# A fused linear-attention and MLP kernel: the first merge of a new block behind the next chunk's products, five constant products, and one group's transposes one step later

## The chip, the cores and the metric

The kernel runs on one core of one Trainium2 chip. The metric is device time in microseconds (us) of one launch; the figure of a version is the median of its runs. The trace comes from one further execution, taken by the hardware profiler. Engines: PE is TensorE (PEld its weight loads), DVE is VectorE, ACT is ScalarE, POOL is GpSimd, SP issues the DMA transfers.

## The reference, cut to what matters

```python
# attention: 4 batches x 8 heads, 768 steps, head size 48
k_n = k / (np.linalg.norm(k, axis=-1, keepdims=True) + 1e-06)
for t in range(S):
    y[:, :, t] = einsum('bhd,bhde->bhe', q[:, :, t], state)
    v_old = einsum('bhde,bhd->bhe', state, k_n[:, :, t])
    state = state + beta[t] * einsum('bhd,bhe->bhde', k_n[:, :, t], v[:, :, t] - v_old)
# first MLP on x [4, 768, 384]
u = x + real(fft(fft(x, axis=1), axis=2))
un = normalized(u)                       # mean 0, variance 1 over 384 features
x = u + max(un @ w_ch1, 0) @ w_ch2       # 384 -> 1536 -> 384
# second MLP with a gate across positions
h = max(x @ w_in, 0);  u, v = halves of h
v_s = w_spatial @ normalized(v) + b_spatial
out = (u * v_s) @ w_out
```

## The kernel before, in words

The recurrence is computed in chunks of 64 steps. There are 4 batches x 12 chunks = 48 chunks, each with all 8 heads, in the order `SEQ` (a new batch begins every four chunks, so several batches are under way at once). A chunk needs the inverse of a triangular 64 x 64 matrix for each head. It is found as two 32 x 32 inverses on DVE (`solve`), for a block of eight chunks at once, and the part below the diagonal is put together by small products on PE (`merge`).

The main loop of `attention` runs over `t` from -3 to 47. One pass holds, on PE, in this order:

- `stage_d(t)`: the output and the new state of chunk t. 32 products take the chunk's values `WU` (the first half), then 32 take the corrected queries `cw` and the state `Sb` (the second half). `cw` is a DVE subtraction in `stage_c`; if it is late, PE stands between the two halves. A chunk that begins a batch has no second half.
- where `t % 8 == 5` and for t = -3 (so at t = -3, 5, 13, 21, 29 and 37): the first merge of a new block, `merge(..., True, False)`: 16 products (L483) on 32 x 32 corners that need `Tc`, the transposed inverses which `solve` writes with two DVE transposes (L352). ACT then writes `ZS` (L487) and copies the diagonal corners (`diag`, L469).
- `stage_c(t+1)`, eight products for the corrections (L532), interleaved pair by pair with `stage_a(t+20)`, eight key products (L224) for a chunk 20 ahead. ACT and DVE copy the result of L224 out (L199, L200). `stage_a` has nothing to do near the end, `stage_c` nothing for a chunk that begins a batch, as for t+1 = 5 and t+1 = 14.
- `stage_b(t+2)` (L517), and at odd t the second part of a merge (L485), which reads `ZS`.

The program's order on each engine is fixed as written (`chain` ties every instruction to the one before it on its engine). The DVE work of `solve` is cut into pieces and spread over the passes by the `part` calls; it is finished at the beginning of the passes t = 13, 21 and 29, just ahead of the merge.

From t = 37 on the Fourier transforms of the finished batches and the conversion of the weights fill in beside the attention. Then follow the first MLP and the second. In the first MLP two groups of 384 positions run interleaved: step `n` is L972 (to the hidden layer), then `between`, then nine products of L985 (back from it). `CF["stats"]` says at which `n` the groups 1 and 2 take their next preparation step, the first tuple of a pair ahead of L972, the second between L972 and L985. A step of group 2 is: statistics, rstd, normalize (`un`, L938 on ACT), then for each of three 128-feature pieces three transposes on PE (L957) and the copies out (L893 on ACT, L894 on DVE).

`halves` holds a helper of its own named `rows` (L413): it multiplies 32 columns of the identity with 288 columns of the mask `mk` and the result is never read.

Of the kernel before, what the change touches and what calls it, by code (L numbers as in the profile page):

```python
# [23 lines left out]
NBC = B * NC  # L24
# [6 lines left out]
HEAD = 24  # L31
# [13 lines left out]
CF = dict(  # L45
    skew=4, ring=20, kq=5, qt=3, mb=2, cvd=3, cve=2, kn=4,
    warm=8, keep=1, last=1, cuts=(0.5, 0.65), dfs=(1, 1, 1, 1, 2, 2, 3, 1, 2, 2, 3, 0), cvt=(0, 0, 0, 1, 2, 2, 1, 1, 0, 0, 0, 0), early=5, first=8, ahead=3,
    turns=(4, 6, 7, 9, 10, 12, 13, 15, 16, 16, 17, 17, 18, 18, 19, 20), stats=(((0, 1, 2, 3, 3), (2,)), ((21, 22, 22), (23, 24, 25))),
)

BANKS0 = dict(X=3, Y=4, Z=1)
# [15 lines left out]
class Kernel:  # L67
# [51 lines left out]
    def attention(self, cp, pg, pe, p, x, filler, after_solves):  # L119
# [345 lines left out]
        def diag(g8):  # L465

            o = (g8 % 4) * 8
            for h, us in enumerate(up):
                (nc.vector.tensor_copy if light(2 * g8 - 3) else nc.scalar.copy)(  # L469
                    out=TT[g8 % NTT][us, :, C * h + 32 : C * h + C], in_=Tts[g8 // 4][us, o : o + 8]  # L470
                )

        def merge(g8, first, second):

            z0, z1 = zz[:, g8 % 2 * 256 : g8 % 2 * 256 + 256].rearrange("p (g n) -> p g n", g=8), zz.rearrange("p (g n) -> p g n", g=8)
            T0, o0 = (Tts[g8 // 4] if first else None), (g8 % 4) * 8
            T1, o1 = (Tts[(g8 - 1) // 4] if second else None), ((g8 - 1) % 4) * 8
            tt = TT[(g8 - 1) % NTT]
            for g in range(8):
                for h in range(2):  # L480
                    if first:
                        ga = gas[g8 * 2 + g // 4][:, g % 4]
                        nc.tensor.matmul(z0[lo[h], g], lhsT=ga[up[h], C : C + 32], rhs=T0[up[h], o0 + g], start=True, stop=True)  # L483
                    if second:
                        nc.tensor.matmul(z1[up[h], g], lhsT=T1[lo[h], o1 + g], rhs=ZS[(g8 - 1) % 2][lo[h], g], start=True, stop=True)  # L485
            if first:
                nc.scalar.mul(ZS[g8 % 2][:96, :, 32:], z0[:96], -1.0)  # L487
            if second:
                for h in range(2):
                    nc.scalar.copy(out=tt[lo[h], :, C * h : C * h + C], in_=z1[up[h]])  # L490
# [31 lines left out]
        def stage_c(bc):  # L522
            qt = qts.pop(bc)
            if SEQ[bc][1] == 0:
                return
            w = st[bc][0]
            cw = p.tile([112, HP, 112], F32, name="cw", bufs=2)
            pc = self.bank("pc", [128, HP, 112])
            for hp in range(HP):
                for h in hs:  # L530

                    nc.tensor.matmul(pc[h, hp], lhsT=w[h, hp, :C], rhs=gas[bc][h, hp, : C + D], start=True, stop=True)  # L532
                yield
            nc.vector.tensor_sub(cw, qt, pc[:112])  # L534
            st[bc][1] = cw

        def stage_d(bc):

            b, c = SEQ[bc]
            wu, cw = st.pop(bc)  # L540
            sb = Sb[b]
            po, ps = self.bank("pd", [128, HP, D]), None
            if c < NC - 1:
                ps = self.bank("pd", [128, HP, D])

            for last in (False, True)[: 1 + (c > 0)]:
                for hp in range(HP):
                    begin, end = (not last and hp == 0, last and hp == HP - 1) if c else (True, True)
                    for i, h in enumerate(hs):

                        k, u, n = (cw[ds[i], hp], sb[ds[i], hp], C + D) if last else (gas[bc][h, hp], wu[h, hp, D:], 2 * C)
                        if ps is not None:
                            nc.tensor.matmul(ps[C * i : C * i + n - C, hp], lhsT=k[:, C:n], rhs=u, start=begin, stop=end)  # L553
                        nc.tensor.matmul(po[hs[1 - i], hp], lhsT=k[:, :C], rhs=u, start=begin, stop=end)  # L554
            if c == HALF:
                px = self.bank("pb", [128, HP, 2, D])
                xr = p.tile([1, DM], F32, name="xr", bufs=2)
                for i in range(2):
                    for hp in range(HP):
                        nc.tensor.matmul(px[C * i : C * i + 1, hp, i], lhsT=qx[ds[i], b, hp : hp + 1], rhs=sb[ds[i], hp], start=True, stop=True)  # L560
            if c < NC - 1:
                nc.scalar.copy(out=sb, in_=ps)
            if c == HALF:
                for i in range(2):
                    nc.scalar.copy(out=xr.rearrange("p (h t d) -> p h t d", h=HP, t=2)[:, :, i], in_=px[C * i : C * i + 1, :, i])
                st["x", b] = xr
            cc = c if c < HALF else NC - 1 - c
            js = slice(64 * (cc % 2), 64 * (cc % 2) + 64)
            tl = cc // 2 + (0 if c < HALF else 3)
            for i in range(2):  # L570
                nc.scalar.copy(out=x[b][js, tl].rearrange("p (h t d) -> p h t d", h=HP, t=2)[:, :, i], in_=po[hs[1 - i]])
            if c == NC - 1:
                nc.scalar.copy(out=x[b][0:1, 3], in_=st.pop(("x", b)))
# [77 lines left out]
        for t in range(T0, NBC):  # L651
            if t in STARTS:
                if solver:
                    solver.finish()
                j, span, total = STARTS[t]
                solver, since = Spread(solve(j), total), t
            part = (lambda f: solver.upto(SECOND(t + f) if j == 1 else (t - since + f) / span)) if solver and not light(t) else (lambda f: None)
            if light(t) and solver:
                solver.finish()
                solver = None  # L660

            if 0 <= t + 2 < NBC and (not light(t) or (t + 2) % 8 == 0) and not sooner(t + 2):
                values(t + 2)
            for bc in ahead.get(t, ()):
                mask_q(bc)
            if t - since < span - 1:
                part(c1)
            if t >= 0:
                stage_d(t)
                if SEQ[t][1] == NC - 1:  # L670
                    fill.extend(filler(SEQ[t][0]))
            new = t % 8 == 5 and t + 3 < NBC
            if new:

                merge((t + 3) // 2, True, False)
                load_kv(t + 3)
                if t >= LAST:
                    load_kv(t + 4)
                diag((t + 3) // 2)
            corrected = stage_c(t + 1) if 0 <= t + 1 < NBC else iter(())  # L680
            if t + R + 2 < HEAD or HEAD <= t + R < NBC:
                stage_a(t + R + 2 * (t < 4), corrected)
            for _ in corrected:
                pass
            if light(t + 1) and t + 3 < NBC and (t + 3) % 8 or sooner(t + 3):
                values(t + 3)
            part(c2)
            odd = t % 2 and (t + 3) // 2 < NBC // 2
            if t == NBC - 12:
                solver.finish()  # L690
                loads, tail = after_solves()
            if t % 2 == 0 and t % 8 != 4 and t + 4 < NBC:
                diag((t + 4) // 2)
            if t < LAST:
                if t % 2 == 0 and t % 8 != 4:
                    merge((t + 4) // 2, True, False)
                if (t + 4) % 8:
                    load_kv(t + 4)
            if (odd or light(t + 1)) and 0 <= t + 2 < NBC:
                stage_b(t + 2)  # L700
            if odd:
                g = (t + 3) // 2
                merge(g + 1, t >= LAST and (g + 1) % 4 > 0, True)
            if light(t + 1):

                for _ in range(CF["dfs"][t - (NBC - 12)]):
                    while fill and next(fill[0], 1) == 1:
                        fill.pop(0)
                for _ in range(CF["cvt"][t - (NBC - 12)]):
                    next(tail, None)  # L710
            elif not odd and 0 <= t + 2 < NBC:
                stage_b(t + 2)
            if t >= LAST and (t + 5) % 8 > 1 and t + 5 < NBC:
                load_kv(t + 5)
            if 2 <= t + 4 < NBC:
                load_qt(t + 4)
            if t == -2:
                right(2)
                left(2)
            if t == -1:  # L720
                right(3)
            if t == 0:
                left(3)
            part(1)

            while late:
                out, m0, m1 = late.pop()
                nc.vector.tensor_tensor(out=out, in0=m0, in1=m1, op=MUL)
            self.chain()
            next(loads, None)  # L730
            if t >= NBC // 2:
                next(self.words, None)
            self.chain()
# [753 lines left out]
```

## Time and profile before

| what | value |
|---|---|
| median of 3 runs | 842.18 us (839.03, 842.18, 850.14) |
| the profiled execution, its own time | 844.23 us |
| its span, first to last instruction | 842.4 us |
| PE busy | 814.1 us, 97% of the span |
| DVE busy | 599.3 us, 71% |
| ACT busy | 408.9 us, 49% |
| mean granted clock of PE | 0.988 |
| chain that ended last | PE 84%, DVE 11%, issue 2% |

The span is what the trace covers; 1.83 us of the execution's own time lie outside it. The granted clock is a share of 2.4 GHz: 1.00 is 2.4 GHz and 0.50 is 1.2 GHz. The attention takes the first 265 us or so of the span; the two MLPs follow.

### The profile page before, as it was taken

The numbers are of one execution on the slowest core, as the hardware profiler recorded it, in microseconds if no ns is written. First come the engines' busy times: TensorE is split into PE (matmuls) and PEld (weight loads), VectorE is DVE, ScalarE is ACT, GpSimd is POOL, SyncE is SP. The second block draws the span as 40 slices with busy tenths as digits, with TensorE's granted clock in tenths as the row PEclk, the third lists the DMA queues.
The fourth block names the chain that finished last, engine by engine and source line by source line (L and its number), as shares of the span: only waits on it lengthen the run. The fifth ranks groups of instructions, "written<-read, shape, count | busy, mean of one in ns | idle before, by whom it ended". The sixth has DMA issues, their size and how long they took to land.

```text
span 842.4 us, 24626 instructions
## 1 busy us (share of the span) xinstructions
PE 814.1 (97%) x10311; PEld 771.2 (92%) x10311; DVE 599.3 (71%) x1715; ACT 408.9 (49%) x1026; POOL 7.6 (1%) x60
## 2 busy tenths in 40 slices
PE   7999999999898999999999999999999999999998
PEld 7778888888787999899999999999999899899998
DVE  6987789999869996682944882346678477586663
ACT  2587878878565543232232551223462453543632
POOL 1000000000000000000000000000000000000000
PEclk9997989999999999999999999999999999999999
DMA  9444545365623300000113210112001101102001
GB/s 232 145 120 113 143 124 142 100 198 154 174 82 134 122 1 1 1 9 21 36 38 118 99 34 18 47 56 59 27 8 47 61 15 43 57 25 61 29 1 57
DMA packets 57441, 62.10 MB, mean 74 GB/s; under 512 B 31793, under 2 KB 48914, under 8 KB 57330
## 3 DMA queue, kind: packets, MB, share of 16 engines
q1 hardware_dynamic: 57186, 60.38, 24.6%
q8 instruction: 81, 1.33, 0.7%
q14 instruction: 30, 0.25, 0.1%
q10 hardware_dynamic: 144, 0.15, 0.1%
HBM read 48.12 MB, written 4.72 MB: 63 GB/s over the span
## 4 chain that ended last, share of the span: by engine, by line
PE 84%; DVE 11%; issue 2%; ACT 1%; DMA 1%; POOL 0%; ACTq 0%; DVEq 0%; POOLq 0%
PE bankX L972 17%; PE bankY L985 15%; PE bankX L1170 10%; PE bankX L1150 6%; PE bankX L1118 6%; PE bankY L1198 5%; PE bankY L517 4%; PE bankX L224 3%; PE bankY L553 2%; PE bankY L532 2%; PE bankV L985 2%; PE bankX L785 2%; PE bankZ L485 2%; PE bankY L554 1%; DVE cw L534 1%
## 5 line engine op out<-in xcount | busy, mean ns | idle before, releaser
L985 PE MATMUL bankY<-w,hx 128*128 128x384 f32 x756 | 147.2, 336 | 0.0
L972 PE MATMUL bankX<-uh,w 128*128 128x384 f32 x504 | 137.6, 340 | 0.7 <-DVE ul L894 0.7
L985 PEld LDWEIGHTS bankY<-w,hx 128*128 128x128 f32 x756 | 132.4, 188 | 0.5 <-issue 0.3
L977 DVE SCALAR_TENSOR_TENSOR hx<-bankX,hx 128x384 fp32r<-128x384 f32 x84 | 46.5, 555 | 75.3 <-ACT hx L976 73.0
L976 ACT ACTIVATE hx<-bankX 128x384 fp32r<-128x384 f32 x84 | 41.1, 490 | 108.6 <-PE bankX L972 104.4
L972 PEld LDWEIGHTS bankX<-uh,w 128*128 128x128 f32 x504 | 92.1, 188 | 1.2 <-DVE ul L894 0.9
L1170 PE MATMUL bankX<-w,A 128*128 128x384 f32 x504 | 88.8, 334 | 0.0
L1170 PEld LDWEIGHTS bankX<-w,A 128*128 128x128 f32 x504 | 87.6, 188 | 0.0
L972 PE MATMUL bankX<-ul,w 128*128 128x384 f32 x252 | 85.1, 338 | 0.0
L517 PE MATMUL bankY<-gak,TT 128*128 128x96 f32 x384 | 57.0, 293 | 1.2 <-issue 0.7
L517 PEld LDWEIGHTS bankY<-gak,TT 128*128 128x128 f32 x384 | 48.9, 199 | 7.6 <-issue 3.0
L1150 PE MATMUL bankX<-xh,s 128*128 128x384 f32 x192 | 50.0, 338 | 0.0
L1159 ACT CAST u<-hx 128x384 fp32r<-128x384 f32 x32 | 15.8, 513 | 67.4 <-DVE hx L1157 67.4
L532 PE MATMUL bankY<-gak,WU 64*64 64x112 f32 x704 | 46.0, 268 | 1.6 <-issue 1.6
L972 PEld LDWEIGHTS bankX<-ul,w 128*128 128x128 f32 x252 | 47.3, 188 | 0.0
L224 PE MATMUL bankX<-kq 48*64 48x128 f32 x640 | 46.5, 287 | 0.6 <-issue 0.5
L1118 PE MATMUL bankX<-s,xh 128*128 128x512 f32 x144 | 45.9, 395 | 0.0
L224 PEld LDWEIGHTS bankX<-kq 48*64 48x64 f32 x640 | 38.6, 143 | 1.8 <-issue 1.1
L1198 PE MATMUL bankY<-s,u 128*128 128x384 f32 x160 | 39.8, 337 | 0.0
L534 DVE TENSOR_TENSOR cw<-qt,bankY 112x448 f32<-112x448 f32 x44 | 27.1, 616 | 17.4 <-PE bankX L224 15.3
L532 PEld LDWEIGHTS bankY<-gak,WU 64*64 64x64 f32 x704 | 35.8, 137 | 2.6 <-issue 2.2
L1150 PEld LDWEIGHTS bankX<-xh,s 128*128 128x128 f32 x192 | 34.8, 188 | 0.2
(242 smaller groups left out, 1766.5 us busy)
## 6 DMA issues: line engine op xcount, KB each, us to landing
qt<-in_qt_dram SPq DMA_DIRECT2D x48, 196.0 KB, 3.3
gak<-in_kv_dram SPq DMA_DIRECT2D x48, 192.0 KB, 4.1
w<-in_w_dram SPq DMA_DIRECT2D x24, 384.0 KB, 5.4
kq<-in_kc_dram SPq DMA_DIRECT2D x12, 448.0 KB, 4.5
out_dram<-x SPq DMA_DIRECT2D x24, 192.0 KB, 1.9
kq<-in_kc_dram SPq DMA_DIRECT2D x16, 224.0 KB, 3.8
x<-x SPq DMA_DIRECT2D x96, 36.0 KB, 1.9
s<-in_wi_dram SPq DMA_DIRECT2D x6, 512.0 KB, 4.7
```

The lines of the kernel that those rows point to most:

```text
L224: nc.tensor.matmul(pa[q, hp], lhsT=kq[r, hp, C:], rhs=kq[r, hp], start=True, stop=True)
L517: nc.tensor.matmul(pb[:, hp].rearrange("p t d -> p (t d)"), lhsT=tt[:, o + hp], rhs=kv[:, hp], start=True, stop=True)
L532: nc.tensor.matmul(pc[h, hp], lhsT=w[h, hp, :C], rhs=gas[bc][h, hp, : C + D], start=True, stop=True)
L534: nc.vector.tensor_sub(cw, qt, pc[:112])
L972: nc.tensor.matmul(ph, lhsT=w1[f][i][:, c * 128 : c * 128 + 128], rhs=cur[k][:, c], start=(c + j == 0), stop=(c == 2 and j == 2))
L976: nc.scalar.activation(hh, ph, AF.Relu)
L977: nc.vector.scalar_tensor_tensor(out=hl, in0=ph, scalar=0.0, in1=hh.bitcast(F32), op0=MAX, op1=SUB)
L985: nc.tensor.matmul(acc[t], lhsT=hx[i][:, t * 128 : t * 128 + 128], rhs=w2[e][k], start=(e == 0 and j == 0), stop=(e == 11 and j == 2),)
L1118: nc.tensor.matmul(pv, lhsT=xT[t][i][:, c, kk * 128 : kk * 128 + 128], rhs=wi[2 * c + 1][k], start=(c + j == 0), stop=(c == 2 and j == 2))
L1150: nc.tensor.matmul(pu, lhsT=wi[2 * c][i][:, f * 128 : f * 128 + 128], rhs=xT[hf][k][:, c], start=(c + j == 0), stop=(c == 2 and j == 2))
L1170: nc.tensor.matmul(acc, lhsT=A[:, m, o, i, kk], rhs=Bo[name, kk][:, k], start=(kk + j == 0), stop=(kk == 2 and j == 2))
L1198: nc.tensor.matmul(po, lhsT=a[:, :128], rhs=wo[f][k], start=(f + j == 0), stop=(f == last and j == 2))
```

## The change

Three parts. First, in the main loop the block `if new:` (merge, loads, `diag`) moves behind `stage_c` and `stage_a` of the same pass. Second, a helper `rows(half, n)` issues n products of 32 constant weight columns with 256 constant columns into the bank of the merges; `stage_d` calls it between its two halves in the passes 3 (one product), 45 (one) and 47 (three). Nothing reads the result. Third, in `CF["stats"]` group 2's fourth preparation step, the first of its three transposes, moves from between L972 and L985 of n = 23 to the head of n = 24.

```diff
-    turns=(4, 6, 7, 9, 10, 12, 13, 15, 16, 16, 17, 17, 18, 18, 19, 20), stats=(((0, 1, 2, 3, 3), (2,)), ((21, 22, 22), (23, 24, 25))),
+    rows={3: (1, 1), 45: (0, 1), 47: (0, 3)},
+    turns=(4, 6, 7, 9, 10, 12, 13, 15, 16, 16, 17, 17, 18, 18, 19, 20), stats=(((0, 1, 2, 3, 3), (2,)), ((21, 22, 22, 24), (24, 25))),
...
+        def rows(half, n):
+
+            for _ in range(n):
+                nc.tensor.matmul(zz[:32, 256 * half : 256 * half + 256], lhsT=self.idn[:, :32], rhs=mk[:, :256], start=True, stop=True)
+
...
             for last in (False, True)[: 1 + (c > 0)]:
+                if last and bc in CF["rows"]:
+                    rows(*CF["rows"][bc])
                 for hp in range(HP):
...
             new = t % 8 == 5 and t + 3 < NBC
+            corrected = stage_c(t + 1) if 0 <= t + 1 < NBC else iter(())
+            if t + R + 2 < HEAD or HEAD <= t + R < NBC:
+                stage_a(t + R + 2 * (t < 4), corrected)
+            for _ in corrected:
+                pass
             if new:
 
                 merge((t + 3) // 2, True, False)
...
                 diag((t + 3) // 2)
-            corrected = stage_c(t + 1) if 0 <= t + 1 < NBC else iter(())
-            if t + R + 2 < HEAD or HEAD <= t + R < NBC:
-                stage_a(t + R + 2 * (t < 4), corrected)
-            for _ in corrected:
-                pass
```

PE before, the pass t = 13, from the last product of the state (L554) to the first product of the next pass (L553, values `WU`); L483 is the first merge, L224 the key products, L517 the next but one chunk's `stage_b`, L485 the second part of a merge:

```order
L554 MATMUL bankY<-Sb_94,cw 64x48
L483 MATMUL bankZ<-Tc,gak 32x32 x16
L224 MATMUL bankX<-kq 64x128 x8
L517 MATMUL bankY<-gak,TT_90 128x96 x4
L485 MATMUL bankZ<-ZS_84,Tc 32x64 x16
L553 MATMUL bankY<-WU_91,gak 64x48
```

PE in the changed kernel, the same pass (lines stand some places lower there: L562 is L554, L225 is L224, L489 is L483, L523 is L517, L491 is L485):

```order
L562 MATMUL bankY<-Sb_94,cw 64x48
L225 MATMUL bankX<-kq 64x128 x8
L489 MATMUL bankZ<-Tc,gak 32x32 x16
L523 MATMUL bankY<-gak,TT_90 128x96 x4
L491 MATMUL bankZ<-ZS_84,Tc 32x64 x16
L561 MATMUL bankY<-WU_91,gak 64x48
```

The merge stands behind the key products, and only L517 is left between it and L485. At t = 5 and 21 what it moves behind is L224 and L532 interleaved, at t = 29 and 37 L532, at t = -3 L224. On ACT `ZS` and `diag` move likewise behind the copies L199 and L200, and on SP the load of a chunk's keys and values behind the load of a key chunk.

PE before, the last pass t = 47, from the corrections of the pass ahead (L532) through nine transposes of the first MLP (L957) to its first product (L972):

```order
L532 MATMUL bankY<-gak,WU_92 64x112 x8
L957 MATMUL bankX<-idn,un 128x128 x9
L554 MATMUL bankY<-WU_92,gak 64x48 x8
L554 MATMUL bankY<-Sb_96,cw 64x48 x8
L972 MATMUL bankX<-uh,w_0_5335 128x384
```

PE in the changed kernel, the same place (L477 is the new `rows`):

```order
L538 MATMUL bankY<-gak,WU_92 64x112 x8
L965 MATMUL bankX<-idn,un 128x128 x9
L562 MATMUL bankY<-WU_92,gak 64x48 x8
L477 MATMUL bankZ<-mk,idn 32x256 x3
L562 MATMUL bankY<-Sb_96,cw 64x48 x8
L980 MATMUL bankX<-uh,w_0_5336 128x384
```

Three constant products stand ahead of the second half.

PE before in the first MLP, from the end of L972 of n = 23 to L972 of n = 24; L957 are group 2's transposes:

```order
L972 MATMUL bankX<-uh,w_10_6467 128x384
L957 MATMUL bankX<-idn,un 128x128 x3
L985 MATMUL bankV<-w_9_6514,xh 128x384 x2
L985 MATMUL bankV<-w_9_6514,xl 128x384
L972 MATMUL bankX<-uh,w_11_6561 128x384
```

PE in the changed kernel, the same place (L993 is L985, L965 is L957, L980 is L972):

```order
L980 MATMUL bankX<-uh,w_10_6472 128x384
L993 MATMUL bankV<-w_9_6519,xh 128x384 x2
L993 MATMUL bankV<-w_9_6519,xl 128x384
L965 MATMUL bankX<-idn,un 128x128 x3
L980 MATMUL bankX<-uh,w_11_6566 128x384
```

The nine products of L985 (the rows of it shown repeat three times) now come ahead of the three transposes, and L972 of n = 24 directly behind them.

## Rows read from the trace of the kernel before

**Rows 1.** Page, busy time and share of the span of each engine

```profile
PE 814.1 (97%) x10311; PEld 771.2 (92%) x10311; DVE 599.3 (71%) x1715; ACT 408.9 (49%) x1026; POOL 7.6 (1%) x60
```

**Rows 2.** PE's waits over the span: us in total, times, longest us

```profile
PE bankY L553 <- DVE cw L534: 3.7, 5, 1.5
...
PE bankZ L483 <- DVE Tc L352: 2.1, 2, 1.1
...
PE bankX L957 <- ACT un L938: 1.5, 3, 1.0
```

**Rows 3.** Windows: stretch, length, busy PE PEld DVE ACT POOL, granted clock, DMA

```profile
69.40:70.80 1.40, 0.44 (x32) 0.32 (x27) 1.37 (x6) 1.36 (x5) 0.15 (x1) 1.00 0.06 15
70.80:81.10 10.30, 10.30 (x162) 9.14 (x154) 7.34 (x44) 5.75 (x21) 0.00 (x0) 0.50 0.24 63
111.80:113.30 1.50, 0.45 (x32) 0.33 (x22) 1.50 (x3) 1.48 (x7) 0.00 (x0) 1.00 0.03 6
...
115.20:122.00 6.80, 6.80 (x128) 6.13 (x129) 4.69 (x29) 3.72 (x11) 0.15 (x1) 0.50 0.60 157
```

**Rows 4.** Timeline, t = 13: start, us, engine, work [idle before, releaser]

```profile
113.33 0.69 PE L483 MATMUL bankZ<-Tc,gak 32*32 32x32 f32 x32 [1.07 <-DVE Tc L352]
...
113.95 1.09 PE L224 MATMUL bankX<-kq 48*64 48x128 f32 x16
```

**Rows 5.** Timeline, t = 21

```profile
150.64 0.69 PE L483 MATMUL bankZ<-Tc,gak 32*32 32x32 f32 x32 [1.06 <-DVE Tc L352]
```

**Rows 6.** Timeline, t = 29

```profile
184.20 0.69 PE L483 MATMUL bankZ<-Tc,gak 32*32 32x32 f32 x32 [0.64 <-DVE w L156]
184.82 0.98 PE L532 MATMUL bankY<-gak,WU 64*64 64x112 f32 x16
185.74 1.13 PE L517 MATMUL bankY<-gak,TT 128*128 128x96 f32 x8
```

**Rows 7.** Windows from one block's transposes to the next: same columns as rows 3

```profile
113.30:150.60 37.30, 34.74 (x1024) 31.29 (x1024) 33.26 (x122) 28.81 (x87) 0.93 (x10) 0.91 0.47 126
150.60:184.20 33.60, 31.91 (x1025) 28.54 (x1025) 32.99 (x122) 27.81 (x84) 0.93 (x10) 1.00 0.52 148
```

**Rows 8.** Timeline, t = -3

```profile
37.93 0.38 ACT L487 ACTIVATE ZS<-bankZ 96x256 f32<-96x256 f32 x1 [0.99 <-PE bankZ L483]
...
38.84 1.08 PE L485 MATMUL bankZ<-ZS,Tc 32*32 32x64 f32 x32
```

**Rows 9.** Costliest groups (busy, mean ns) and timeline: the constant product of 288 columns

```profile
L413 PE MATMUL bankY<-mk,idn 128*32 128x288 f32 x20 | 6.7, 418 | 0.0
...
34.87 0.67 PE L413 MATMUL bankY<-mk,idn 128*32 128x288 f32 x2
```

**Rows 10.** Timeline, `stage_d` of t = 3, 45 and 47

```profile
65.58 0.24 PE L553 MATMUL bankY<-Sb,cw 48*48 48x48 f32 x1 [0.50 <-DVE cw L534]
...
255.38 0.60 DVE L534 TENSOR_TENSOR cw<-qt,bankY 112x448 f32<-112x448 f32 x1
...
263.03 0.62 DVE L534 TENSOR_TENSOR cw<-qt,bankY 112x448 f32<-112x448 f32 x1
...
264.59 0.63 PE L554 MATMUL bankY<-Sb,cw 48*64 48x48 f32 x16
265.15 0.44 PE L972 MATMUL bankX<-uh,w 128*128 128x384 f32 x1
```

**Rows 11.** Timeline, n = 23 of the first MLP

```profile
347.35 1.90 ACT L938 ACTIVATE un<-x,l1n,l1r 128x384 f32<-128x384 f32 x3 [1.25 <-DVE l1n L932]
348.11 0.33 PE L957 MATMUL bankX<-idn,un 128*128 128x128 f32 x1 [0.98 <-ACT un L938]
...
349.39 0.59 PE L985 MATMUL bankV<-w,xh 128*128 128x384 f32 x2
...
349.66 0.56 DVE L977 SCALAR_TENSOR_TENSOR xl<-bankX,xh 128x384 fp32r<-128x384 f32 x1 [0.95 <-ACT xh L976]
...
351.04 0.34 PE L972 MATMUL bankX<-uh,w 128*128 128x384 f32 x1
```

## The prediction

> **What bounds the kernel now.** I read the page first: PE is busy for 97% of the span and DVE for 71% [rows 1], so time can come only out of PE's few waits, out of work on PE, or out of stretches in which PE runs at half clock. Next the list of PE's waits in the attention: the first merges wait for `Tc`, the state products for `cw` [rows 2]. Then the windows, for the clock: in the main loop it is 1.00 except for two stretches, 70.8 to 81.1 us (10.3 us) and 115.2 to 122.0 us (6.8 us), where it is 0.50, the lower level of 1.2 GHz; before the first PE had 0.44 us of work in 1.40 us, before the second 0.45 us in 1.50 us, then the light products of a first merge [rows 3]. Last the same windows for DVE. From one block's transposes to the next it is busy for 33.26 of 37.3 us and for 32.99 of 33.6 us [rows 7]: in the second of these the inverses on DVE set the pace as much as PE does, and a microsecond that PE saves there is waited for again at the next `Tc`. That is the reason why I don't simply add up the waits.
>
> **Moved merge, the waits.** At t = 13, 21 and 29 PE stands for 1.07, 1.06 and 0.64 us ahead of the merge, until DVE has finished the transposes [rows 4 to 6], 2.77 us in all. What now comes first needs no `Tc`: at t = 13 L224 (1.09 us), at t = 29 L532 (0.92 us from its start to that of L517), at t = 21 both interleaved (I take 1.0 us) [rows 4, 6]. So each wait is covered but for some 0.1 us, seen from the transposes. Seen along the loop they aren't added: relative to `Tc` PE is 1.0 us ahead after t = 13, and again 1.0 us after t = 21, but to keep both DVE must reach the second `Tc` 1.0 us sooner. It is idle for 4.04 us before t = 21 (2.11 us of them in the slow stretch [rows 3]) and for 0.61 us before t = 29 [rows 7]. I let DVE come 0.5 us sooner in the first, outside the slow stretch, and 0.3 us in the second, about half of the 0.61 us; with 0.98 us of cover at the last of the three that is **1.8 us**. Bounds: 0.98 us (DVE gains nothing) and 2.77 us (all three waits go). The list of waits has no other for `Tc` [rows 2], so at t = 5 and 37 nothing is gained. What hides the merge's later end: L485 needs `ZS`, which takes ACT 0.38 us [rows 8], and L517 (1.13 us [rows 6]) still lies between; if ACT came later than that, L485 would wait. That cover is missing at t = -3 alone: in the trace `ZS` is ready at 38.31 us, 0.53 us ahead of L485 [rows 8]; now L485 follows the merge directly, and ACT has the copies of L224's result to do ahead of `ZS`. I put **+0.2 us**, bounds 0 and 1.0 us. The loads on SP go past one load each and their data are used three passes later: nothing. DVE's order is the same but at t = 37, where two copies change places with a subtraction: nothing.
>
> **Moved merge, the clock.** The stretch at 0.50 from 115.2 us begins right behind the merge that had waited, with PE idle for most of the 1.5 us ahead of it [rows 3]. Without that idle time I expect this fall not to come. It costs PE half of 6.8 us, 3.4 us, since PE is busy through all of it; but DVE has only 6.80 - 4.69 = 2.11 us idle there, and the next `Tc` comes no sooner than that. So the clock gives **2.1 us**, bounds 0 and 3.4 us. The earlier stretch begins in t = 4, behind a wait of 0.96 us for `cw` that the change leaves alone; the product in t = 3 lies one pass ahead of it. I count nothing for it.
>
> The Trainium skill speaks against this term: "TensorE: Matmul & The Clock Gate", section "HAM oscillation — how this bites in real kernels", tells of a clock that falls in long waits for data, which waits of 1.1 us are not; by it the fall isn't bought back by filling this wait. The trace agrees with it in part only: the clock did fall, behind a wait of 1.07 us, but I can't show that the wait was what made it fall. By that page the clock gives 0 and the sum below ends 2.1 us higher.
>
> **The constant products.** The trace has products of the same kind with 288 columns. One is two records, 0.67 us from the first start to the last end, at 0.418 us each [rows 9], so that they follow each other by 0.25 us. Scaled by 256/288 the new one costs 0.60 us at most; two times the spacing makes it 0.44 us, which I take, since a record's end overlaps what follows. In t = 3 it lies in a wait of 0.50 us [rows 10]: free. In t = 45 `cw` is ready at 255.98 us [rows 10] and the list of waits shows no long one there: of 0.44 us I let 0.2 us stick out. In t = 47 there is no wait at all: `cw` is ready at 263.65 us and its products start at 264.59 us, directly behind the first half, and the first MLP's L972 directly behind them [rows 10]. Three products there are 3 x 0.44 = 1.32 us on PE's path. Together **+1.5 us**, bounds 0 (if the waits of the passes before, or of the transposes after, take them up) and 5 x 0.60 = 3.0 us. The one long wait for `cw` in this part, 1.5 us [rows 2], lies in t = 46, where no product is put.
>
> **The transposes.** At n = 23 PE waits three times for the pieces of `un`, 1.5 us in all and 0.98 us the first time, and ACT finishes the last at 347.35 + 1.90 = 349.25 us [rows 2, 11]. Nine products of L985 (349.39 to 351.04 us, 1.65 us) now run in that time. But L972 of n = 24 needs a bank that DVE has read out only at 349.66 + 0.56 = 350.22 us, and ACT and DVE work in the same order as before. So L972 starts at 350.25 us and not at 351.04 us: **0.8 us**, bounds 0 and 1.5 us.
>
> **The sum.** Profiled execution 844.23 us - 1.8 + 0.2 - 2.1 + 1.5 - 0.8 = 841.2 us. That execution lies 844.23 - 842.18 = 2.05 us above the median, and the runs shown spread over 11 us, which the waits alone don't explain; a slow stretch that comes in one execution and not in another would. So I take the difference, -3.0 us, to the median: **839.2 us**, 0.4% less.
>
> **Rivals.** (1) The clock falls as before, or falls a pass later, and only waits are gained: -0.9 us, 841.3 us. For it: nothing shows what lets the clock fall, and the 10.3 us stretch begins where the change does nothing. Against it: both falls come behind a stretch with PE idle for two thirds of it. (2) Both stretches go, because the product in t = 3 and the dense products at t = 5 help: DVE has 10.30 - 7.34 = 2.96 us idle in the first, so 2.96 us more, 836.2 us, down to 834 us if DVE doesn't bind (half of 10.3 us is 5.15 us). For it: at t = 5 the merge lay inside the slow stretch. Against it: the stretch begins earlier. (3) Slower: the first merge, L517 and L485 now follow each other at t = 13, 21 and 29, with no key products or corrections among them, so that light products are gathered, and the clock falls behind them. Each such fall costs half of 6.8 us; t = 13 keeps its own, t = 21 and t = 29 get one each: 841.3 + 2 x 3.4 = 848.1 us. It decides as soon as the clock is 0.50 behind L485 at t = 21 or 29. Against it: L517 is a full-width product and was there before. (4) The change doesn't do what it says for the products: they aren't in waits, and t = 47 pays for all three. That is in the sum; were they hidden it would be 837.7 us, inside the forecast's own range.
>
> **How the numbers follow.** The forecast, 837 to 841 us, gets 0.42; rival 1, 841 to 843.5 us, 0.27; rival 2, 833 to 837 us, 0.20; rival 3, 845 us and more, 0.08; 0.03 for anything else. The range from 833 to 847 us holds the first three and the nearer half of the slower case. A measurement of this kernel can tell about 2% from no change, 16.8 us, so 825.3 and 859.0 us are the limits. All cases but accidents lie within: same 0.96, faster 0.02, slower 0.02.
>
> **What the changed profile would show.** Right: no wait of L483 over 0.3 us at t = 13, L483 directly ahead of L517; at t = 29 a wait of at most 0.5 us; clock 1.00 from 111 to 122 us; L972 of n = 24 some 1.7 us after the end of L985; the three products at t = 47 with no idle time ahead of them and L972 1.3 us later after `stage_d` begins. Wrong: a granted clock of 0.50 at t = 13 again (rival 1), none between 40 and 260 us (rival 2), or one at t = 21 or 29 (rival 3); L485 waiting for ACT at any of the six passes; a wait for `cw` in t = 14, 22 or 30 that takes back what the merge gave.

## The result

The changed kernel takes **852.06 us** (median of 21 runs, 845.38 to 859.01) against 843.79 us before (21 runs beside them, 837.53 to 855.98). The ratio is **1.0106, 95% interval 1.0083 to 1.013**: some 9 us slower, where 3 us less were forecast. (Ratios leave out the executions that are over 1.5% above the fastest of their kernel; medians and mean clocks take all runs.) The profiled execution took 855.65 us.

The page of the changed kernel: span, busy times (beside [rows 1]) and the granted clock in 40 slices of 21 us.

```profile
span 853.9 us, 24651 instructions
...
PE 828.9 (97%) x10321; PEld 783.1 (92%) x10321; DVE 599.4 (70%) x1715; ACT 409.5 (48%) x1026; POOL 7.6 (1%) x60
...
PEclk8958987999999999999999999999999999999999
```

PE is busy for 14.8 us more, with ten records more; DVE and ACT do the same work as before. So PE was slower, not idler. The windows of the changed kernel show where; columns as in [rows 3].

```profile
36.00:45.20 9.20, 7.51 (x206) 5.89 (x204) 9.20 (x49) 5.81 (x20) 0.00 (x0) 1.00 0.49 131
45.20:69.10 23.90, 23.90 (x524) 18.80 (x522) 13.54 (x48) 12.30 (x39) 0.00 (x0) 0.50 0.21 59
93.00:96.40 3.40, 3.40 (x97) 3.07 (x93) 0.10 (x1) 2.42 (x8) 0.00 (x0) 0.50 0.02 5
123.70:137.30 13.60, 13.60 (x245) 12.36 (x244) 9.31 (x52) 8.06 (x23) 0.15 (x1) 0.50 0.41 112
232.90:236.30 3.40, 3.40 (x81) 3.23 (x82) 3.31 (x14) 0.92 (x3) 0.00 (x0) 0.50 0.94 275
263.60:267.00 3.40, 3.40 (x46) 3.12 (x37) 3.40 (x8) 0.94 (x3) 0.00 (x0) 0.51 0.23 64
```

Those are 47.7 us at 1.2 GHz, where before had 17.1 us in the main loop [rows 3] (both have a few more ahead of 22 us). The largest, 23.9 us, lies in the passes behind t = -3. The same stretch of before has the clock at 1.00:

```profile
45.20:69.10 23.90, 22.80 (x747) 19.30 (x748) 20.78 (x57) 18.98 (x63) 0.77 (x9) 1.00 0.45 124
```

It holds 747 products where the changed kernel gets through 524. At before's rate those 524 would take 23.9 x 524/747 = 16.8 us: an estimate of 7.1 us for this stretch alone.

What stands ahead of it is the merge of t = -3. The timeline of the changed kernel there (SPq are the DMAs of SP's queue):

```profile
38.56 0.69 PE L489 MATMUL bankZ<-Tc,gak 32*32 32x32 f32 x32
...
39.07 4.08 SPq L106 DMA_DIRECT2D gak<-in_kv_dram  x3
...
39.34 0.39 ACT L493 ACTIVATE ZS<-bankZ 96x256 f32<-96x256 f32 x1
...
39.79 1.08 PE L491 MATMUL bankZ<-ZS,Tc 32*32 32x64 f32 x32 [0.54 <-ACT ZS L493]
...
43.35 1.01 ACT L513 ACTIVATE gak<-gak,n_all 128x48 f32<-128x48 f32 x4 [1.26 <-DMA gak<-in_kv_dram]
43.73 1.14 PE L523 MATMUL bankY<-gak,TT 128*128 128x96 f32 x8 [0.90 <-ACT gak L513]
```

And of before, the load and its users:

```profile
37.67 0.69 SPq L105 DMA_DIRECT2D gak<-in_kv_dram  x1
...
42.03 1.01 ACT L507 ACTIVATE gak<-gak,n_all 128x48 f32<-128x48 f32 x4 [0.89 <-DMA gak<-in_kv_dram]
...
42.42 1.14 PE L517 MATMUL bankY<-gak,TT 128*128 128x96 f32 x8 [0.53 <-ACT gak L507]
```

L491 now waits 0.54 us for `ZS`. And the load of chunk 0's keys and values starts 1.4 us later (39.07 instead of 37.67 us): `stage_b` of the next pass waits 0.90 us instead of 0.53 us. PE's long waits in the rest of the attention, from the changed kernel's list of waits (us in total, times, longest):

```profile
PE bankY L561 <- DVE cw L540: 2.7, 4, 1.5
...
PE bankZ L489 <- issue: 1.4, 1, 1.4
...
PE bankX L225 <- issue: 1.1, 1, 1.1
...
PE bankZ L477 <- ACT ZS L493: 0.5, 1, 0.5
...
PE bankZ L489 <- DVE Tc L353: 0.2, 1, 0.2
```

The waits for `Tc` are down to 0.2 us, as intended [rows 2].

### The profile page after: what moved, and what is told of

It reads as the page before. It is cut to its first block, busy times and chain, and to the rows that moved or that the text cites. A ratio compares the mean times of both kernels' runs of the same rounds, so it can differ in the third digit from the quotient of the medians.

```text
span 853.9 us, 24651 instructions
## 1 busy us (share of the span) xinstructions
PE 828.9 (97%) x10321; PEld 783.1 (92%) x10321; DVE 599.4 (70%) x1715; ACT 409.5 (48%) x1026; POOL 7.6 (1%) x60
## 4 chain that ended last, share of the span: by engine, by line
PE 87%; DVE 7%; ACT 2%; issue 2%; DMA 0%; POOL 0%; ACTq 0%; DVEq 0%; POOLq 0%
PE bankX L980 17%; PE bankY L993 15%; PE bankX L1178 10%; PE bankX L1158 6%; PE bankX L1126 6%; PE bankY L1206 5%; PE bankY L523 5%; PE bankX L225 3%; PE bankY L561 3%; PE bankY L538 2%; PE bankZ L491 2%; PE bankY L562 2%; PE bankX L793 2%; PE bankV L993 2%; PE bankZ L489 1%
## 5 line engine op out<-in xcount | busy, mean ns | idle before, releaser
L993 PE MATMUL bankY<-w,hx 128*128 128x384 f32 x756 | 147.2, 336 | 0.0
L980 PE MATMUL bankX<-uh,w 128*128 128x384 f32 x504 | 137.8, 340 | 1.3 <-DVE ul L902 0.7
L993 PEld LDWEIGHTS bankY<-w,hx 128*128 128x128 f32 x756 | 132.4, 188 | 0.5 <-issue 0.3
L985 DVE SCALAR_TENSOR_TENSOR hx<-bankX,hx 128x384 fp32r<-128x384 f32 x84 | 46.2, 551 | 76.7 <-ACT hx L984 74.2
L980 PEld LDWEIGHTS bankX<-uh,w 128*128 128x128 f32 x504 | 92.1, 188 | 2.0 <-DVE ul L902 0.9
L980 PE MATMUL bankX<-ul,w 128*128 128x384 f32 x252 | 85.1, 338 | 0.0
L523 PE MATMUL bankY<-gak,TT 128*128 128x96 f32 x384 | 59.6, 302 | 1.5 <-ACT gak L513 0.9
L523 PEld LDWEIGHTS bankY<-gak,TT 128*128 128x128 f32 x384 | 51.2, 207 | 7.8 <-issue 3.0
L538 PE MATMUL bankY<-gak,WU 64*64 64x112 f32 x704 | 48.5, 281 | 1.7 <-issue 1.3
L225 PE MATMUL bankX<-kq 48*64 48x128 f32 x640 | 48.2, 299 | 1.1 <-issue 1.1
L980 PEld LDWEIGHTS bankX<-ul,w 128*128 128x128 f32 x252 | 47.3, 188 | 0.0
L225 PEld LDWEIGHTS bankX<-kq 48*64 48x64 f32 x640 | 40.5, 150 | 2.1 <-issue 1.5
L538 PEld LDWEIGHTS bankY<-gak,WU 64*64 64x64 f32 x704 | 38.6, 146 | 2.5 <-issue 1.6
L562 PE MATMUL bankY<-WU,gak 64*64 64x48 f32 x768 | 35.3, 233 | 0.8 <-issue 0.8
```

The lines of the kernel that those rows point to most:

```text
L225: nc.tensor.matmul(pa[q, hp], lhsT=kq[r, hp, C:], rhs=kq[r, hp], start=True, stop=True)
L523: nc.tensor.matmul(pb[:, hp].rearrange("p t d -> p (t d)"), lhsT=tt[:, o + hp], rhs=kv[:, hp], start=True, stop=True)
L980: nc.tensor.matmul(ph, lhsT=w1[f][i][:, c * 128 : c * 128 + 128], rhs=cur[k][:, c], start=(c + j == 0), stop=(c == 2 and j == 2))
L985: nc.vector.scalar_tensor_tensor(out=hl, in0=ph, scalar=0.0, in1=hh.bitcast(F32), op0=MAX, op1=SUB)
L993: nc.tensor.matmul(acc[t], lhsT=hx[i][:, t * 128 : t * 128 + 128], rhs=w2[e][k], start=(e == 0 and j == 0), stop=(e == 11 and j == 2),)
```

## The experiments

Theory A: the moved merge of t = -3 leaves PE with too little to do in a light stretch, and the clock falls there for long. Rivals: the constant products cost the time (B), the later merges gather light work (C), the order of transfers or of products does it (D, E), or chips and hours do (F). Every set ran on another chip, with before beside it. "Clock" is the mean granted clock over all timed runs, kernel / before. Within one kernel's runs the time follows the clock: a line through the runs of all kernels (each with its own height) gives 6.6 us for 0.01. "Equal clock" is the difference of the mean times after both are moved along that line to 0.985 (standard errors 0.4 to 0.8 us).

| set | kernel | median, before | ratio, 95% interval | clock | equal clock |
|---|---|---|---|---|---|
| 1 | merge | 847.67, 844.12 | 1.003 (0.9989 to 1.007) | .979 / .985 | +0.8 |
| 1 | rows | 845.64 | 1.0014 (0.9977 to 1.0051) | .986 | +2.1 |
| 1 | turns | 848.11 | 0.9982 (0.9936 to 1.0029) | .979 | -0.5 |
| 1 | m3stay | 843.90 | 0.9992 (0.9953 to 1.003) | .988 | +1.3 |
| 2 | m3only | 858.71, 848.13 | 1.0118 (1.0066 to 1.017) | .966 / .980 | -0.2 |
| 2 | fill | 854.12 | 1.0067 (1.0027 to 1.0107) | .981 | +6.0 |
| 2 | best1 | 844.54 | 0.9983 (0.9941 to 1.0026) | .982 | -2.2 |
| 3 | again | 853.24, 851.01 | 0.999 (0.9945 to 1.0036) | .978 / .976 | +2.1 |
| 3 | fill2 | 855.37 | 1.0011 (0.9952 to 1.007) | .977 | +4.4 |
| 3 | stall | 846.66 | 0.998 (0.9936 to 1.0025) | .982 | +0.4 |
| 3 | best2 | 849.41 | 0.9941 (0.9888 to 0.9993) | .983 | +1.6 |
| 4 | again2 | 855.22, 846.16 | 1.0116 (1.0072 to 1.016) | .973 / .979 | +1.7 |
| 4 | m3stay2 | 843.59 | 0.999 (0.9953 to 1.0027) | .985 | 0.0 |
| 4 | m3only2 | 855.17 | 1.0133 (1.0085 to 1.0181) | .971 | +0.8 |
| 4 | best3 | 844.76 | 1.0009 (0.9969 to 1.0049) | .986 | -0.1 |
| 5 | stall2 | 857.07, 844.85 | 1.0134 (1.0082 to 1.0186) | .971 / .982 | +0.8 |
| 5 | fill3 | 852.32 | 1.0082 (1.004 to 1.0124) | .976 | +1.8 |

**One part at a time.** `merge` is the changed kernel without the products and with the old `stats`; `rows` and `turns` are before with one part each:

```diff
-    rows={3: (1, 1), 45: (0, 1), 47: (0, 3)},
+    rows={},
```

> Only the first merges of the six new blocks are moved; no constant products, transposes as before. Theory A (the loss is the clock, and the moved merges bring it, above all the one at t = -3, which now makes PE wait for ZS and leaves a longer half-clock stretch in the early passes): 849 to 852 us, ratio 1.006 to 1.010, mean granted clock about 0.975. Rival B (the five constant products and their waits cost the time): 841 to 843 us, ratio 0.997 to 1.000, clock as before.

> Only the five constant products are added. Theory A: the products cost 1.3 to 1.7 us, 845 us, ratio 1.002. Rival B (the products bring the loss): 850 us and more, ratio 1.008.

> Only group 2's first transposes move from n = 23 to the head of n = 24. Theory A: 0.8 us gained, 843 us, ratio 0.999. Rival: the new wait for the bank at n = 24 costs as much as the transposes gave, 0.0 us, ratio 1.000.

The products cost 2.1 us at equal clock and leave the clock alone; the transposes gain 0.5 us. `merge` is 3.6 us above before in the median, less than A wanted, and its interval holds 1. The spread within a set is large: `turns` does nothing in the attention, and its clock came out at .979.

**The merge of t = -3.** `m3stay` is the changed kernel with this one merge left in place, `m3only` is before with it alone moved:

```diff
             new = t % 8 == 5 and t + 3 < NBC
+            if new and (t < 0):
+
+                merge((t + 3) // 2, True, False)
...
-            if new:
+            if new and not (t < 0):
```

> The changed kernel, but the merge of the pass t = -3 stays ahead of the key products as before. Theory A (the early merge is the cause): the loss goes, 842 to 845 us, ratio 0.998 to 1.002, and no half-clock stretch of over 10 us between 40 and 70 us. Rival C (the merges of t = 13, 21 and 29 behind the key products gather light work and let the clock fall): 849 to 852 us, ratio 1.007 to 1.010, with the stretch at t = 13 still there.

> The kernel before with the merge of t = -3 alone moved. Theory A (this move is the cause: PE then waits for ZS and for the keys and values that are loaded later, and the half-clock stretch follows in the early passes): mean clock 0.974 to 0.980, 848 to 852 us, ratio 1.005 to 1.009, waits of about 0.5 us for ZS and 0.9 us for the scaled values. Rival C (it needs the other moved merges, or the products, as well): clock 0.984 and 844 to 846 us.

> The changed kernel itself once more, beside the others on one chip. All theories: clock 0.973 to 0.978, ratio 1.008 to 1.013.

> The changed kernel, on one chip with the three others of this set. Theory A (the merge of t = -3 in its new place costs the clock): mean clock 0.006 to 0.014 below that of the kernel with this merge kept in place, and a half-clock stretch of over 15 us from about 45 us on in the profiled execution. Rival F (the falls of the clock are chance, and the earlier difference was one of chips and hours): clocks equal within 0.003.

> The changed kernel with the merge of t = -3 in its old place, once more. Theory A: the clock of the kernel before or up to 0.004 higher, 4 to 8 us less than the changed kernel beside it. Rival F: within 2 us of the changed kernel.

> The kernel before with the merge of t = -3 alone moved, once more. Theory A: clock 0.006 to 0.014 below before on the same chip, 4 to 9 us more than before. Rival F: within 2 us of before.

`m3only` and `m3only2` lose 1.2% and 1.3% with a clock 0.0146 and 0.0085 below before; `again2` lies 0.0117 below `m3stay2` beside it, 11.6 us more in the median. At equal clock these kernels differ from their counterparts by -0.2 to +1.7 us. So C falls, B but for its 2.1 us, and F as the whole cause: this one merge brings the loss, and through the clock. How large the loss is differs: against before, `merge` lies 0.0060 lower in clock and `again2` 0.0063. And set 3 is an exception: before had a low clock itself (.976) there and `again` was level with it; why is not settled. Of 133 timed runs of before 30 had a clock of .99 or more; of 69 runs with this merge moved and no dense products behind it, 2.

The profiled executions agree. With the merge moved all seven have a half-clock stretch of 17 to 31 us beginning between 35 and 46 us; with it in place one of nine has (`m3stay2`). One window of four kernels, `again2`, `m3only2`, `m3stay` and `m3stay2`:

```profile
45.00:60.00 15.00, 15.00 (x280) 11.04 (x279) 4.26 (x18) 6.81 (x21) 0.00 (x0) 0.50 0.33 86
```

```profile
45.00:60.00 15.00, 15.00 (x307) 11.07 (x310) 5.33 (x24) 7.21 (x24) 0.00 (x0) 0.50 0.33 83
```

```profile
45.00:60.00 15.00, 14.15 (x466) 11.40 (x464) 12.43 (x44) 11.62 (x40) 0.00 (x0) 1.00 0.34 96
```

```profile
45.00:60.00 15.00, 15.00 (x299) 11.07 (x302) 5.04 (x22) 6.14 (x19) 0.00 (x0) 0.50 0.35 86
```

The fourth row is a reminder: the same fall comes without the move too, only seldom. And in `again2` the clock is 0.50 from 36 us on, ahead of the moved merge, so that there the move didn't begin it.

**Which wait.** `kvfirst` loads the chunk ahead of the key products again. The load overwrites columns that the merge reads, so its result differs and only its time is read; for the same reason the load can't be left in place in the real kernel.

```diff
+            if new and t < 0:
+                load_kv(t + 3)
...
-                load_kv(t + 3)
+                if t > 0:
+                    load_kv(t + 3)
```

> The changed kernel, but at t = -3 the load of the next chunk's keys and values stays ahead of the key products; merge and diagonal copies stay moved. Theory A1 (the late load makes the longer wait, and the clock hangs on it): the wait for the scaled values falls from 0.9 to 0.4 us, mean clock 0.983 to 0.988, 844 to 847 us. Theory A2 (the wait for ZS, and the light merge products that follow each other, are enough): clock 0.975, 850 to 853 us.

852.17 us (6 runs, clock .978) beside 848.13. Its L523 no longer waits, and the clock falls all the same, at about 39 us, behind the wait for `ZS`:

```profile
38.60 1.38 PE L491 MATMUL bankZ<-ZS,Tc 32*32 32x64 f32 x32 [0.54 <-ACT ZS L493]
...
39.91 1.97 PE L225 MATMUL bankX<-kq 48*64 48x128 f32 x16
...
42.80 0.53 PE L523 MATMUL bankY<-gak,TT 128*128 128x96 f32 x1
```

(L225 takes 1.97 us for what takes 1.09 us in [rows 4].) So the late load isn't needed for the fall: A1 fails as the whole cause, and in this execution A2 holds. What the load adds stays open: one of the six runs took 837.35 us at a clock of .996, the mean clock is only 0.0026 below before, and `m3only`, on the same chip and with the late load, came out at .966.

**Idle time or order.** `stall` and `stall2` keep before's order and put four or seven copies on ACT ahead of `ZS`:

```diff
+                if g8 == 0:
+                    dm = p.tile([128, 256], F32, name="dm", bufs=1)
+                    for _ in range(7):
+                        nc.scalar.copy(out=dm, in_=mk[:, :256])
                 nc.scalar.mul(ZS[g8 % 2][:96, :, 32:], z0[:96], -1.0)
```

> The kernel before, with nothing moved, but four copies of ACT (about 0.4 us each, into a tile that nothing reads) ahead of ZS at t = -3, so that PE waits there about 1 us with its own order as before. Theory A (idle time in this light stretch is what costs the clock): against before on the same chip the clock is 0.006 to 0.012 lower and the time 5 to 9 us higher, with a half-clock stretch of over 10 us between 40 and 70 us. Rival E (the order of the products, light ones one behind another, costs the clock, not the wait): clock as before, 0.5 to 1 us more.

> The kernel before, nothing moved, with seven instead of four copies of ACT ahead of ZS at t = -3. The four copies made PE wait only 0.24 us for ZS and 0.72 us for TT; three more of 0.43 us should make it 1.5 us for ZS. Theory A (idle time there costs the clock): a half-clock stretch of over 15 us from about 40 us on, mean clock 0.006 to 0.014 below before on the same chip, 5 to 10 us more. Rival E (the order of the light products costs the clock, not idle time): clock as before, 1 to 2 us more.

Four copies were too few: ACT had been idle there, and PE stood for 0.24 and 0.72 us.

```profile
38.56 1.08 PE L485 MATMUL bankZ<-ZS,Tc 32*32 32x64 f32 x32 [0.24 <-ACT ZS L491]
...
41.38 0.69 PE L483 MATMUL bankZ<-Tc,gak 32*32 32x32 f32 x32 [0.72 <-ACT TT L494]
```

That run is inconclusive: before waits 0.25 and 0.53 us at the same place, so that little was added, and it ran in set 3, where the changed kernel lost nothing either. Seven copies, with nothing moved, bring the loss: 1.0134, clock 0.0103 below before. So a late `ZS`, and what follows it on ACT, is enough without the new order. How long PE stood there is not known: the profiled execution of `stall2` took 1979.64 us and isn't read here, nor in the clock. (The other five ran from 848.34 to 858.37 us, with a median of 856.63 us.)

That doesn't exclude rival E for the move itself, and the amount of idle time alone doesn't explain the fall. Three windows of about the same work, up to the first product of the `stage_b` of t = -2, in before, in the changed kernel and in `best1` (this merge in place):

```profile
26.00:42.42 16.42, 14.73 (x450) 10.36 (x447) 15.32 (x59) 8.18 (x28) 0.93 (x10) 1.00 0.43 124
```

```profile
27.00:43.73 16.73, 15.03 (x453) 10.66 (x449) 15.16 (x59) 8.27 (x29) 0.93 (x10) 1.00 0.47 135
```

```profile
27.00:43.57 16.57, 14.56 (x449) 10.26 (x443) 15.09 (x59) 8.36 (x28) 0.93 (x10) 1.00 0.44 114
```

PE is idle for 1.69, 1.70 and 2.01 us in them, and the clock falls right behind the second alone (at 45.2 us). What differs is the place: in before 0.91 us of the idle time lies ahead of the merge's last products and 0.78 us behind them, in the changed kernel all that is listed (0.54, 0.24 and 0.90 us) lies behind the merge. Whether this place or the order of the light products lowers the clock, no run separates.

**Dense work in the wait.** Constant products behind the moved merge: in `fill` two at t = -3 and two ahead of the next `stage_b`, in `fill2` four at t = -3, in `fill3` (which is `m3only`) two.

```diff
+                if t == -3:
+                    rows(1, 2)
                 merge(g + 1, t >= LAST and (g + 1) % 4 > 0, True)
```

> The changed kernel with four more constant products, two in the wait for ZS at t = -3 and two in the wait for the scaled values at t = -2; nothing else differs. Theory A (the clock falls because PE has too little to do there): clock 0.984 to 0.990 and 844 to 848 us, although four products are added. Rival D (the loss comes from the order of the transfers or from something that dense products do not change): clock 0.975 and 852 to 854 us.

> The changed kernel with four more constant products between the merge of t = -3 and the second part that waits for ZS; nothing behind it, so that no product waits for a later ZS. They take 4 x 0.45 = 1.8 us, of which the waits for ZS (0.5 us) and for the scaled values (0.9 us) should hide most. Theory A (the clock falls because PE has too little work there): against the changed kernel on the same chip the mean clock is 0.006 to 0.012 higher and the time 4 to 7 us lower. Rival D (something else about the moved merge): clock the same, time 0 to 1 us higher.

> The kernel before with the merge of t = -3 alone moved, and two constant products (0.9 us) in the wait for ZS that this makes. Without them this kernel took 1.2% and 1.3% more than before on two chips, with a clock 0.009 to 0.015 lower. Theory A (too little work on PE there): clock within 0.004 of before, 0 to 3 us more than before. Rival D (dense products there don't bring the clock back): clock 0.009 to 0.015 lower, 8 to 11 us more.

None of the three profiles has the long stretch (`fill` has 3.4 us of it); that of `fill3`:

```profile
38.43 1.05 PE L477 MATMUL bankZ<-mk,idn 128*32 128x256 f32 x4 [0.55 <-ACT ZS L493]
...
39.41 1.08 PE L491 MATMUL bankZ<-ZS,Tc 32*32 32x64 f32 x32
...
42.42 1.14 PE L523 MATMUL bankY<-gak,TT 128*128 128x96 f32 x8
```

The products don't go into the wait: they write the bank that `ZS` is copied from, wait for `ZS` themselves, and come behind it. In `fill` the second pair waits 2.96 us for the next `ZS`, which explains most of its +6.0 us. The mean clocks are mixed: `fill` level with before, `fill2` level with `again`, `fill3` 0.0055 below before, between A and D. That dense work brings the clock back is possible, not shown, and it doesn't pay.

**A better version.** `best1` keeps only the later merges and the transposes. `best2` adds products where `cw` is waited for; `best3` has as many in a bank of their own (the lower part of the diff).

```diff
-    rows={3: (1, 1), 45: (0, 1), 47: (0, 3)},
+    rows={3: (0, 1), 4: (0, 2), 45: (0, 1), 46: (0, 3)},
...
-                    rows(*CF["rows"][bc])
+                    own = self.bank("pa", [128, 256])
+                    for _ in range(CF["rows"][bc]):
+                        nc.tensor.matmul(own[:32], lhsT=self.idn[:, :32], rhs=mk[:, :256], start=True, stop=True)
```

> Merge of t = -3 and products as before, the later merges and the transposes as in the changed kernel. Theory A: no loss of clock (0.985 to 0.988), the parts that gain are left: 841 to 843 us, ratio 0.996 to 0.999. Rival C (the later merges lower the clock): 845 us and more.

> Merge of t = -3 as before, the later merges and the transposes as changed, and constant products where the waits for cw are: one at t = 3, two at t = 4, one at t = 45, three at t = 46. Theory A (dense work in waits keeps the clock, and costs nothing where the wait is as long): clock 0.986 to 0.992, 838 to 842 us on a chip on which before takes 844 us, ratio 0.992 to 0.997. Rival B (the products stick out, as at t = 47): 844 to 846 us.

> The kernel with the merge of t = -3 in place, later merges and transposes as changed, and constant products in the waits for cw at t = 3 (one), 4 (two), 45 (one) and 46 (three), now in a bank of their own from the key products' pool, so that no product waits for ZS or TT. Theory A: they fit into the waits of 0.5, 0.96, 0.6 to 0.9 and 1.1 to 1.5 us, so that at equal clock it is 1 to 3 us below before, and the clock is 0.003 to 0.008 higher: ratio 0.990 to 0.996. Rival B (they stick out all the same): at equal clock 0 to 2 us above before, ratio 0.996 to 1.000.

`best1` is 2.2 us below before at equal clock, which its ratio can't resolve. `best2` is faster on its chip (0.9941), all of it by the clock (.983 against .976), since at equal clock its products cost: at t = 4 they wait for `TT` and then stick out.

```profile
69.61 1.05 PE L477 MATMUL bankZ<-mk,idn 128*32 128x256 f32 x4 [0.65 <-ACT TT L496]
```

`best3` has the highest clock of its set and a ratio of 1.0009. `best3` beats the changed kernel beside it (855.22 us); that `best2` lies below its own (853.24 us) is within the spread of the runs. None of the three is shown to beat before on more than one chip.

## Why the prediction was wrong

**The step that failed** is the account of t = -3. "The loads on SP go past one load each and their data are used three passes later: nothing" is wrong there: chunk 0's keys and values are used in the next pass. (So are the loads at the other five places, where PE shows no wait of 0.5 us or more for them.) "+0.2 us" for `ZS` measured 0.54 us, within its bounds. But the price of these waits is not their length. I gave a fall of the clock a price at t = 13, where a wait goes, and none at t = -3, where one is added. On the three comparisons that show it most clearly (`m3only` and `m3only2` against before, `again2` against `m3stay2`: 0.0146, 0.0085, 0.0117) the move costs 0.0116 of clock, at 6.6 us for 0.01 some 7.7 us; with the +1.9 us at equal clock of `again` and `again2` that is 9.6 us, against some 9 us measured. The other comparisons give less (0.0060 for `merge`, 0.0063 for `again2` against before, none in set 3), so that the near agreement is in part a matter of which are taken. By what means the move lowers the clock, the place of the wait or the order of the light products, stays open.

**Moved merge, the waits (-1.8 us).** The waits for `Tc` went as said (0.2 us at t = 21, none at t = 29). In the loop they gave little or nothing. `Tc`'s transposes, in `turns` (merge ahead) and `m3stay` (behind), both with the clock at 1.00 there:

```profile
107.01 1.94 DVE L353 STREAM_TRANSPOSE Tc<-Ts 128x512 f32<-128x512 f32 x2
...
141.46 1.93 DVE L353 STREAM_TRANSPOSE Tc<-Ts 128x512 f32<-128x512 f32 x2
...
175.24 1.93 DVE L353 STREAM_TRANSPOSE Tc<-Ts 128x512 f32<-128x512 f32 x2
```

```profile
111.56 1.95 DVE L353 STREAM_TRANSPOSE Tc<-Ts 128x512 f32<-128x512 f32 x2
...
146.23 1.96 DVE L353 STREAM_TRANSPOSE Tc<-Ts 128x512 f32<-128x512 f32 x2
...
179.79 1.97 DVE L353 STREAM_TRANSPOSE Tc<-Ts 128x512 f32<-128x512 f32 x2
```

From the second to the third are 33.78 and 33.56 us; two more executions with the clock at 1.00 there have 33.51 us (`stall`, merge ahead) and 33.58 us (`best1`, behind). So DVE sets the pace there, and of the 0.3 us by which I let it come sooner next to nothing came. From the first to the second the four have 34.45 and 35.76 us (ahead), 34.67 and 34.97 us (behind): the spread is as large as my 0.5 us, which is not shown. What PE gains it gives back two passes ahead of the third `Tc`, waiting for `cw`, which stands in DVE's queue among the inverses; in the changed kernel:

```profile
185.05 0.61 DVE L540 TENSOR_TENSOR cw<-qt,bankY 112x448 f32<-112x448 f32 x1
...
185.72 0.24 PE L561 MATMUL bankY<-Sb,cw 48*48 48x48 f32 x1 [1.48 <-DVE cw L540]
```

The prediction named such a wait as a sign of error, in t = 30, not here. By the traces, what is left is mainly the 0.98 us at the last of the three. The runs can't tell that from my 1.8 us: at equal clock, with the products and the transposes taken at 2.1 and 0.5 us, `best1` gives the later merges 1.7 us, `m3stay` 0.3 us and `m3stay2` 1.6 us, with standard errors of 0.6 to 0.9 us.

**Moved merge, the clock (-2.1 us).** The fall behind t = 13's merge came again, at 123.7 us, and lasted 13.6 us. In place of the wait for `Tc` PE stood 1.08 us for nothing that the profile shows, ahead of the key products:

```profile
121.76 0.87 PE L225 MATMUL bankX<-kq 48*64 48x128 f32 x12 [1.08 <-issue]
...
122.56 0.69 PE L489 MATMUL bankZ<-Tc,gak 32*32 32x32 f32 x32
```

Rival 1 was right in this. Rival 3 had the mechanism, falls behind gathered light work, and nearly the time (848.1 us), but the wrong place: no fall came at t = 21 or 29 in this execution. The Trainium skill, "TensorE: Matmul & The Clock Gate", section "HAM oscillation — how this bites in real kernels", tells of falls in long waits for data. The trace goes further: in `kvfirst` the clock fell behind a wait of 0.54 us between light products (which need not be its only cause).

**The products (+1.5 us)** were mis-sized in one term: 2.1 us at equal clock. At t = 47 the three took 276.67 - 275.26 = 1.41 us, as said. At t = 3 the product is not free: it waits for `ZS` as long as the state products had waited for `cw`, and then adds its own length.

```profile
75.90 0.62 PE L477 MATMUL bankZ<-mk,idn 128*32 128x256 f32 x2 [0.51 <-ACT ZS L493]
...
275.26 1.48 PE L477 MATMUL bankZ<-mk,idn 128*32 128x256 f32 x6
...
276.67 0.67 PE L562 MATMUL bankY<-Sb,cw 48*64 48x48 f32 x16
```

**The transposes (-0.8 us)** did what was said. L980 of n = 24 starts 2.92 us after `un` begins, where L972 started 351.04 - 347.35 = 3.69 us after [rows 11], and what ends its wait is the bank:

```profile
359.47 1.91 ACT L946 ACTIVATE un<-x,l1n,l1r 128x384 f32<-128x384 f32 x3 [1.25 <-DVE l1n L940]
...
362.39 0.44 PE L980 MATMUL bankX<-uh,w 128*128 128x384 f32 x1 [0.64 <-DVE xl L985]
```

That is 0.77 us in this execution, 0.5 us (standard error 0.5 us) in the runs of `turns`.

## What to carry to other kernels

When a step moves, ask at every one of its places what it is late for, its loads too, and look hardest at the place with the least cover: here five of the six places were harmless and the sixth cost more than all others could give. Price a new wait by what the clock does behind it, not by its length, and be wary of one among light products. And where another engine sets the pace of a loop, expect a wait that is taken away inside it to come back at that engine's next result.

## What the runs showed of the hardware

The mean granted clock of one and the same kernel, before, ranged from .949 to .998 over 133 runs, the time from 835.55 to 869.45 us; one profile says little about it. In the changed kernel the falls at 93.0, 123.7, 232.9 and 263.6 us each begin within 2 us of a wait of 0.88 to 1.40 us, while the longest wait, 1.48 us at 185.72 us, has no fall behind it. Waits for nothing that the profile shows stand at the same places of PE's program in most executions, with another length each time: that in L538 (L532 of before), 219 to 232 us into the span, was 1.12 us in before, 1.34 us in the changed kernel and 2.25 us in `m3stay`.
